# Token sums of batches 1 to 7 as seven block products, with their weights read from DRAM through a ring

## The chip, the cores and the metric

The kernel runs on one core of a Trainium2 chip. The core has a matrix engine (PE; its weight loads are listed apart as PEld), a vector engine (DVE), a scalar engine (ACT), a general engine (POOL, GpSimd), and SP, which here only issues DMAs. Each engine works through its own instructions in order; semaphores make one wait for another. The metric is the time on the device in microseconds (us), the median of several runs.

## The reference

For each of 8 batches of x (3008 tokens, 256 channels, fp32):

```python
# filter
X = np.fft.rfft(x, axis=1)
x = np.fft.irfft(X * (filt_r + 1j * filt_i), n=3008, axis=1)
# mixer
xt = x.transpose(0, 2, 1)
h = np.maximum(xt @ w_tok1, 0.0) @ w_tok2       # 3008 -> 256 -> 3008, over the tokens
u = x + h.transpose(0, 2, 1)
out = u + np.maximum(u @ w_ch1, 0.0) @ w_ch2     # 256 -> 1536 -> 256, over the channels
```

The change concerns `xt @ w_tok1`, the sums over the tokens, for batches 1 to 7.

## The kernel before

**Stages.** The filter is a discrete Fourier transform split into factors (`dft`). It runs for groups of batches, (0), (1, 2), (3, 4), (5, 6), (7); its result goes to DRAM (`g_tmp`) and comes back as six tiles `t4[b, c]` for each batch (`t4_load`), each with 4 of 24 blocks of 128 rows by 256 channels. The blocks are in a space in which one more small transform is still to be done; `w1` holds w_tok1 in that same space, 24 blocks of 128 rows by 256 columns, and stays in SBUF for the whole program.

**The mixer's loop** (`mix`). Its items are (batch, m, jp): m counts 6 groups of up to 512 tokens, jp 6 pairs of blocks of the 1536 hidden channels, so a batch has n = 36 items, 288 in all. An item has three places (0, 1, 2). The up and down products are already made as seven block products each (`up_first`, `up_last`, `down`): sums of the operands on DVE, seven matmuls on PE, sums of the products on ACT and DVE. In place 0 an item issues `up_first` (four matmuls on `ps_pg`, then ACT's copy to `s`), `up_middle` (two adds on DVE), the previous item's `h_sums` (three operations on DVE that write `t`) and the first half of its `down`. In place 1 it issues `up_last` (three matmuls, then DVE's adds into `hh` and ACT's relus), in place 2 the second half of the previous item's `down`, which reads `t`. A finished m adds `finish` to a list of steps (`todo_v`), taken one at a time; the last of these turns the result and stores it with DMAs from POOL (L950).

**The token sums.** At item 32 of a batch (n - 4), place 2, `token_sums(b + 1)` runs 48 matmuls of 128x128 weights by 256 columns into one bank of PSUM (L746), and `token_relu` applies relu on ACT (L754) and has POOL make the five combinations (`combine`) that the second product needs. Their first use is in item 34 (`u_quarter`, L790). Before item 0 of batch 0, `token_sums(0)` does the same for batch 0.

**Around it.** The matmuls of `u_filter` (L768) move 128 columns each. The weights of the second product go to DRAM during batch 0 (`w2_sums` on POOL, one step for each item from item 8) and are loaded for each m again (`w2m_load` on SP, L809). The filter's units for the next group are placed between the mixer's places by a table of due places; their DVE work (L669, L674, L675) and matmuls (L518) lie among the mixer's. They use the two banks `acc` and `b`, as the token sums and the u parts do.

**Order.** The program's order is written out by hand (manual schedule): each engine does its instructions in the order in which they are issued here, and waits come from data and buffers. The pool of the t4 tiles has seven buffers. SP issues most loads, also of the filter's tables and of z.

Of the kernel before, what the change touches and what calls it, by code (L numbers as in the profile page):

```python
# [10 lines left out]
FP32 = mybir.dt.float32  # L11
I64 = mybir.dt.int64
U32 = mybir.dt.uint32
AF = mybir.ActivationFunctionType
ALU = mybir.AluOpType


B = 8
# [5 lines left out]
P = 128  # L24
# [24 lines left out]
W2G = -(-N2 // NG)  # L49
PARTS = (0, 64, 96, 112)  # L50
BY_PE = 6
IN_B = 16
EARLY = 12
GROUPS = ((0,), (1, 2), (3, 4), (5, 6), (7,))
# [71 lines left out]
def kernel(  # L126
# [26 lines left out]
                 for g, bs in enumerate(GROUPS)] for what, shape in (("z", (P, A)), ("g", (K2, KR))))  # L153

    w2_d = nc.dram_tensor("w2_tmp", (MT, P, 7, 256), FP32, kind="Internal").ap()

    def pool(name, bufs, **kw):
        return ctx.enter_context(tc.tile_pool(name=name, bufs=bufs, **kw))
# [38 lines left out]
    filts = [glob.tile([P, 2, KC, D], FP32, name="filt%d" % i) for i in range(FB)]  # L197

    filts_0 = list(filts)
    w1 = glob.tile([P, A, DT], FP32, name="w1")  # L200

    w2 = glob.tile([P, TC, A * P], FP32, name="w2")

# [117 lines left out]

        behind.append(f)

    def w1_load(i):
        st = stage(512)
        rows = moe_w_tok1.rearrange("(n2 n1) t -> n2 n1 t", n1=N1)
        q = nc.sync if i < EARLY else nc.gpsimd
        last = 2 * i + 2 == A
        if last:
            nc.gpsimd.memset(st.bitcast(U32)[HALF:P, 512:1024], 0)  # L330
        for h in range(2):
            n = 1 if last and h else 2
            lo = h * A + 2 * i
            src = rows[:, lo:lo + n, :]
            if h == 0:
                src = bass.AP(tensor=rows.tensor, offset=rows.offset + (A - 1 - lo) * DT,
                              ap=[[N1 * DT, N2], [-DT, n], [1, DT]])
            q.dma_start(st[h * HALF:(h + 1) * HALF, 0:n * DT].rearrange("p (a t) -> p a t", t=DT), src)
        yield

        h = halves(st, 512, spare_pair())
        yield next(h)
        yield next(h)
        on_chip(wai_t, *next(h), 512, [(lambda v: v, w1[:, 2 * i:2 * i + 2, :].rearrange("p a t -> p (a t)"))])

    def w2_load(i):

        t, g = divmod(i, W2G)
        nn = min(NG, N2 - g * NG)
        n = nn * N1  # L350

        st = stage(512)
        nc.gpsimd.dma_start(st[:, 0:n], moe_w_tok2[ts(t, P), ds(g * NG * N1, n)])
        yield
        dst = w2[:, t].rearrange("p (a h n2) -> p h n2 a", h=2, n2=HALF)[:, :, ds(g * NG, nn), :]

        def some(h, first, step, w):
            return (lambda v: bass.AP(tensor=v.tensor, offset=v.offset + first, ap=[v.ap[0], [N1, nn], [step, w]]),
                    dst[:, h, :, 0:w])

        parts = [some(0, A - 1, -1, A), some(1, A, 1, A - 1)]
        if i < BY_PE:
            h = halves(st, n, spare_pair())
            yield next(h)
            yield next(h)
            on_chip(ident, *next(h), n, parts)
        else:
            yield from rounded(st, n, parts, False)

    def combine(w):  # L370
        a11, a12, s4, na22, s3, s2, s1 = (w[:, :, n, :] for n in range(7))
        add = nc.gpsimd.tensor_tensor
        nc.gpsimd.tensor_scalar(out=na22, in0=s1, scalar1=-1.0, scalar2=None, op0=ALU.mult)
        add(out=s1, in0=s3, in1=s1, op=ALU.add)
        add(out=s3, in0=a11, in1=s3, op=ALU.subtract)
        add(out=s2, in0=s1, in1=a11, op=ALU.subtract)
        add(out=s4, in0=a12, in1=s2, op=ALU.subtract)  # L377
# [16 lines left out]
    def wc2_load(i):  # L394
# [11 lines left out]
        while put_off:  # L406
# [4 lines left out]
    LAST = ((wc2_load, 0), (wc1_load, 1), (wc1_load, 4), (wc2_load, 1), (wc1_load, 2), (wc2_load, 2), (wc1_load, 5),  # L411
            (wc2_load, 3), (wc2_load, 4), (wc2_load, 5))

    tiles = ([w1_load(i) for i in range(A // 2)] + [w2_load(i) for i in range(TC * W2G)]
             + [wc1_load(c * (DC // 512), False) for c in range(DH)] + [f(i) for f, i in LAST])
    begin, copy, middle, end = (iter(tiles) for _ in range(4))

# [27 lines left out]
    def copies():  # L445

        while copied[0] < len(tiles) and copied[0] <= ended[0] + 1:
            advance(copy)
            copied[0] += 1
# [292 lines left out]
    def token_sums(b):  # L742
# [4 lines left out]
                                 start=(a == 0 and t == 0), stop=(a == A - 1 and t == TC - 1))  # L747
        return acc

    def token_relu(b, acc):  # L750
        if b:
            h1 = w2[:, 0:1, 7 * 256:].rearrange("p o (s t) -> p o s t", t=P)[:, :, 0:7, :]
            for t, to in enumerate((slice(0, 5, 4), slice(1, 7, 5))):
                nc.scalar.activation(out=h1[:, 0, to, :], in_=acc[:, t].rearrange("p (e i) -> p e i", e=DH), func=AF.Relu)  # L754
            combine(h1)
            return h1[:, 0]
        h1 = h1p.tile([P, TC, D], FP32, tag="h1", name="h1")
        nc.scalar.activation(out=h1, in_=acc, func=AF.Relu)
        return h1
# [86 lines left out]
    def v(out, in0, in1, op=ALU.add):  # L846
        nc.vector.tensor_tensor(out=out, in0=in0, in1=in1, op=op)  # L847
# [127 lines left out]
    def one_step():  # L975
        if todo_v:
            todo_v.pop(0)()

    def mix(next_ready):

        wait = []
        pos, hhs, tts = {}, {}, {}

        def loads(b):
            if b + 1 < B and next_ready(b):
                for c in wait:
                    t4_load(b + 1, c)
                wait.clear()


        own = ({(4, 2): (0, 1)}, {(3, 0): (0,), (4, 0): (1,), (4, 2): (2, 3)})
        new = {(JP - 2, 0): (0, 1), (JP - 1, 0): (2, 3)}

        def u_parts(b, m, jp, place):
            parts = own[b > 0] if m + 1 < MT else new if b + 1 < B else {}
            now = parts.get((jp, place), ())
            b, m = (b, m + 1) if m + 1 < MT else (b + 1, 0)
            for part in now:
                u_part(b, m, part)
            if now and now[-1] == max(p for ps in parts.values() for p in ps):  # L1000
                if m:
                    wait.append(m)
                todo_v.extend(v_steps(b, m))
                if b and (b, m) < (B - 1, MT - 2):
                    w2m_load((m + 2) % MT)

        to_dram = [f for m in range(MT) for f in w2_sums(m)]
        items = [(b, m, jp) for b in range(B) for m in range(MT) for jp in range(JP)]
        n = MT * JP
        for i in range(len(items) + 1):  # L1010
            now, old = i < len(items), i >= 1
            if i and ended[0] < len(tiles):
                convert_middle()
                convert_end(False)
                convert_middle()
            if now:
                b, m, jp = items[i]
                if i % n == 0:
                    wait.append(0)
                w = width(m)  # L1020
                hhs[i] = hp.tile([P, 4, 256], FP32, tag="hh", name="hh")
                g = [bank("pg").rearrange("p (s n) -> p s n", s=2) for _ in range(2)]
                s = up_first(jp, uts[b, m], vts[b, m], w, g)
                up_middle(hhs[i], w, g, s)
            one_step()
            if old:
                bo, mo, jo = items[i - 1]
                tts[i - 1] = tp.tile([P, 4, 256], FP32, tag="t", name="t")
                for f in h_sums(hhs[i - 1], tts[i - 1], width(mo)):
                    f()  # L1030
                down(mo, jo, 0, hhs[i - 1], tts[i - 1], pos.setdefault((bo, mo), []))
            if now:
                u_parts(b, m, jp, 0)
            copies()
            yield b, i % n, 0
            if ended[0] < len(tiles):
                if i == 0:
                    convert_middle()
                convert_end(False)
            if now:  # L1040
                up_last(jp, uts[b, m], vts[b, m], w, g, s, hhs[i])
            one_step()
            if now and i % n == n - 1:
                one_step()
            copies()
            loads(b)
            yield b, i % n, 1
            if old:
                down(mo, jo, 1, hhs.pop(i - 1), tts.pop(i - 1), pos[bo, mo])
                if jo == JP - 1:  # L1050
                    todo_v.extend(finish(bo, mo, uts[bo, mo], pos[bo, mo]))
                    one_step()
                    one_step()
            if now:
                if b + 1 < B and i % n == n - 4:
                    h1s[b + 1] = token_relu(b + 1, token_sums(b + 1))
                u_parts(b, m, jp, 2)
                if jp == JP - 1:
                    while todo_v and m + 1 == MT:
                        one_step()  # L1060
                if i >= 8 and to_dram:
                    to_dram.pop(0)()
                if i in (28, 29):
                    w2m_load(i - 28)
            loads(b)
            yield b, i % n, 2
        while todo_v:
            one_step()
# [125 lines left out]
```

## Time and profile before

| what | value |
|---|---|
| median of three runs (lowest, highest) | 2458.51 us (2456.95, 2459.57) |
| the profiled execution: its time, its span | 2459.61 us, 2457.5 us |
| granted TensorE clock, mean over the span | 0.996 |
| token sums of batches 1 to 7 (L746), first matmul to the next other one, each | 20.7 us |
| DVE's busy share | 75% |
| DMA: moved in all, mean rate | 234.50 MB, 95 GB/s |

The page gives each engine's busy time as a share of the span, the chain of work that ended last, and the costliest groups of instructions with their mean duration and the idle time in front of them. A row of the timeline is: start, length in us, engine, line, operation, what is written and read, shape and count, and in brackets the idle time before it with what ended it. An fp32 matmul stands in the records as two passes, each with a weight load of its own, so the 48 matmuls of a block are 96 records.

### The profile page before, as it was taken

How to read it: one execution, taken by the hardware profiler on the slowest of the kernel's cores; microseconds unless marked ns; L12 is line 12 of the kernel's file. 1: busy time of each engine (PE TensorE's matmuls, PEld its weight loads, DVE VectorE, ACT ScalarE, POOL GpSimd, SP SyncE). 2: the span in 40 equal slices, each digit the busy share in tenths (PEclk: the TensorE clock that was granted, in tenths of full speed). 3: DMA queues.
4: the chain of work that ended last, by engine and by line, in shares of the span. 5: the costliest groups of instructions: out<-in, count | busy, mean ns of one | idle time of the engine just before them, and what ended most of it. 6: DMA issues, size and time to landing. Idle time of an engine off the chain costs nothing.

```text
span 2457.5 us, 33961 instructions
## 1 busy us (share of the span) xinstructions
PE 2413.4 (98%) x11836; PEld 1967.7 (80%) x11836; DVE 1845.0 (75%) x3404; ACT 685.1 (28%) x1348; POOL 601.5 (24%) x1091
## 2 busy tenths in 40 slices
PE   7999999999999999999999999999999999999998
PEld 4767766978788877887888878897888888898887
DVE  7797788587876788578875887857785788757776
ACT  5733222132222222123221222213221222212222
POOL 8483322122112211211211122112212112112121
PEclk8999999999999999999999999999999999999999
DMA  9974434353332232245332322323322121201100
GB/s 217 245 231 130 128 114 137 107 160 107 111 89 59 74 85 57 88 126 159 97 92 57 86 80 73 103 58 116 102 63 73 50 71 47 96 24 30 39 15 20
DMA packets 173842, 234.50 MB, mean 95 GB/s; under 512 B 34013, under 2 KB 123819, under 8 KB 173672
## 3 DMA queue, kind: packets, MB, share of 16 engines
q1 hardware_dynamic: 128856, 174.02, 24.1%
q0 software_dynamic: 33216, 48.32, 7.8%
q10 hardware_dynamic: 11600, 10.00, 1.3%
q8 instruction: 94, 1.54, 0.3%
q14 instruction: 76, 0.62, 0.1%
HBM read 154.99 MB, written 77.22 MB: 94 GB/s over the span
## 4 chain that ended last, share of the span: by engine, by line
PE 88%; DVE 6%; DMA 3%; issue 1%; ACT 1%; POOL 0%; DVEq 0%; ACTq 0%; SPq 0%; POOLq 0%
PE ps_po L903 33%; PE ps_pg L869 18%; PE ps_pg L885 14%; PE ps_b L746 3%; PE ps_acc L746 3%; PE ps_b L518 3%; PE ps_b L790 3%; PE ps_acc L790 2%; PE ps_acc L518 2%; PE ps_b L768 2%; PE ps_acc L768 2%; DVE t L847 1%; DVE hh L847 1%; DVE p L669 1%; DVE u L847 1%
## 5 line engine op out<-in xcount | busy, mean ns | idle before, releaser
L950 POOL DMA_DIRECT2D out_dram<-r x752 | 409.6, 553 | 1646.5 <-ACT hh L890 1433.7
L847 DVE TENSOR_TENSOR hh<-ps_pg,s 128x512 f32<-128x512 f32 (+3 forms) x864 | 482.4, 586 | 384.3 <-ACT s L872 379.8
L890 ACT ACTIVATE hh<-hh 128x512 f32<-128x512 f32 (+1 forms) x576 | 347.8, 621 | 963.1 <-DVE hh L847 956.3
L903 PE MATMUL ps_po<-t,wc 128*128 128x256 f32 (+1 forms) x2304 | 546.5, 380 | 4.6 <-DVE t L847 3.5
L903 PEld LDWEIGHTS ps_po<-t,wc 128*128 128x128 f32 x2304 | 426.5, 190 | 129.8 <-DVE t L847 44.1
L903 PE MATMUL ps_po<-hh,wc 128*128 128x256 f32 (+1 forms) x1728 | 414.0, 375 | 1.4 <-POOL wc L377 0.8
L869 PE MATMUL ps_pg<-v,wc 128*128 128x256 f32 (+1 forms) x1728 | 413.5, 375 | 0.1
L903 PEld LDWEIGHTS ps_po<-hh,wc 128*128 128x128 f32 x1728 | 326.4, 190 | 42.7 <-ACT s L872 3.9
L869 PEld LDWEIGHTS ps_pg<-v,wc 128*128 128x128 f32 x1728 | 326.8, 190 | 40.9 <-DVE v L847 2.9
L885 PE MATMUL ps_pg<-u,wc 128*128 128x256 f32 (+1 forms) x1152 | 295.2, 379 | 0.6 <-DVE hh L847 0.6
L885 PEld LDWEIGHTS ps_pg<-u,wc 128*128 128x128 f32 x1152 | 214.9, 190 | 57.5 <-DVE hh L847 23.7
L847 DVE TENSOR_TENSOR t<-t,hh 128x256 f32<-128x256 f32 (+1 forms) x576 | 245.1, 426 | 19.8
L847 DVE TENSOR_TENSOR s<-ps_pg,hh 128x512 f32<-128x512 f32 (+1 forms) x288 | 196.1, 681 | 31.4 <-DVE hh L847 1.8
L872 ACT COPY s<-ps_pg 128x256 f32<-128x256 f32 (+1 forms) x288 | 106.0, 368 | 330.4 <-PE ps_pg L869 327.6
L847 DVE TENSOR_TENSOR t<-hh 128x512 f32<-128x512 f32 (+1 forms) x288 | 194.9, 677 | 0.6 <-ACT hh L890 0.6
L869 PE MATMUL ps_pg<-u,wc 128*128 128x256 f32 (+1 forms) x576 | 171.7, 380 | 3.4 <-DVE hh L847 3.3
L885 PE MATMUL ps_pg<-v,wc 128*128 128x256 f32 (+1 forms) x576 | 168.8, 375 | 0.0
L869 PEld LDWEIGHTS ps_pg<-u,wc 128*128 128x128 f32 x576 | 106.8, 190 | 35.5 <-DVE hh L847 20.1
L885 PEld LDWEIGHTS ps_pg<-v,wc 128*128 128x128 f32 x576 | 109.2, 190 | 12.6
L847 DVE TENSOR_TENSOR u<-ps_b,u 128x256 f32<-128x256 f32 (+2 forms) x102 | 58.3, 572 | 67.3 <-PE ps_b L790 61.8
L847 DVE TENSOR_TENSOR u<-ps_acc,u 128x512 f32<-128x512 f32 (+2 forms) x108 | 62.4, 577 | 55.8 <-PE ps_acc L790 51.5
L746 PE MATMUL ps_b<-t,w 128*128 128x256 f32 x384 | 85.3, 385 | 1.9 <-DMA t<-g_tmp 1.9
(135 smaller groups left out, 2483.4 us busy)
## 6 DMA issues: line engine op xcount, KB each, us to landing
w<-w_tmp SPq DMA_DIRECT2D x35, 896.0 KB
out_dram<-r POOLq DMA_DIRECT2D x696, 32.0 KB, 2.4
t<-g_tmp SPq DMA_DIRECT2D x42, 512.0 KB
g_tmp<-t SPq DMA_DIRECT2D x96, 192.0 KB
t<-z_tmp SPq DMA_DIRECT2D x180, 96.0 KB
z_tmp<-t SPq DMA_DIRECT2D x60, 256.0 KB
filt<-in_x_dram SPq DMA_DIRECT2D x90, 128.0 KB
wb<-wbi_t SPq DMA_DIRECT2D x64, 128.0 KB
```

What stands on the lines that cost most here:

```text
L518: nc.tensor.matmul(outs(i, j), stat(i, j), mov(i, j), start=True, stop=True)
L669: nc.vector.tensor_tensor(out=prods[c, h], in0=pss[h].unsqueeze(1).to_broadcast([P, 2, nb, D]), in1=filts[c % FB][:, :, 0, :].unsqueeze(2) ...
L746: nc.tensor.matmul(acc[:, t, :], w1[:, a, ts(t, P)], t4[b, a // TC4][:, a % TC4, :], start=(a == 0 and t == 0), stop=(a == A - 1 and t == ...
L768: nc.tensor.matmul(ps[:, ds(q * P, n)], t4[b, c][:, r, ts(dh, P)], wai[:, 0:n], start=(first and q == 0), stop=(not first and q == 3))
L790: nc.tensor.matmul(ps[:, ds(j * hw, hw)], h1[:, n, :], w2m[m % 2][:, at, 0:hw], start=(i < 2 and j == 0), stop=(j == len(todo) - 1))
L847: nc.vector.tensor_tensor(out=out, in0=in0, in1=in1, op=op)
L869: nc.tensor.matmul(ps[:, 0:hw], chan[0][:, jp, n, :], mov, start=True, stop=True)
L872: nc.scalar.copy(out=s[:, 0], in_=g[0][:, 0, 0:hw])
L885: nc.tensor.matmul(ps[:, 0:hw], chan[0][:, jp, n, :], mov, start=True, stop=True)
L890: nc.scalar.activation(out=hs, in_=hs, func=AF.Relu)
L903: nc.tensor.matmul(po[i][:, j, 0:hw], chan[1][:, jp, n, :], mov, start=(jp == 0 and first == 1), stop=(jp == JP - 1 and last == 1))
L950: q.dma_start(bass.AP(tensor=ob.tensor, offset=ob.offset + row * D + g * cw, ap=[[N1 * D, 32], [D if h else -D, n], [1, cw]]), blocks[ts(g ...
```

## The change

For batches 1 to 7 the token sums are formed as 12 steps. A step j takes two blocks of rows of the tokens (2j and 2j + 1), in two halves of channels each, and the two times two 128x128 blocks of `w1` that belong to them, and makes seven products of 128x128 by 128 columns (`token_product`) in place of four of 128x128 by 256, which are eight of 128. Four of the moving operands are sums made on DVE (`t4_sums`, three operations for a step, into a tile with two slots that comes from the pool of the t4 tiles); steps 0 and 1 are issued in place 1 of item 32, step j + 2 right after the matmuls of step j. The products add up over the steps in parts of both banks `acc` and `b`, and at the end ACT copies one part and four DVE operations combine the parts into a tile `c` (from the pool of `r`), before ACT's two relus and POOL's `combine` as before.

The seven weight blocks of a step are in DRAM (`w1_tmp`): from item 8 of batch 0 on, `w1_sums` writes the unchanged blocks out, makes the four combinations in place with 16 operations on POOL, and writes these. They come back through a ring of seven slots in the place that `w1` had (`w1_load`, SP): seven in items 25 to 31, one in place 1 of each, and the last five inside the product, each after the step whose slot it takes. Batch 0 still uses `token_sums`.

```diff
@@ -49,6 +49,8 @@
 W2G = -(-N2 // NG)
 PARTS = (0, 64, 96, 112)
 BY_PE = 6
+AP = A // 2
+W1S = 7
 IN_B = 16
 EARLY = 12
 GROUPS = ((0,), (1, 2), (3, 4), (5, 6), (7,))
@@ -153,6 +155,7 @@
                  for g, bs in enumerate(GROUPS)] for what, shape in (("z", (P, A)), ("g", (K2, KR))))
 
     w2_d = nc.dram_tensor("w2_tmp", (MT, P, 7, 256), FP32, kind="Internal").ap()
+    w1_d = nc.dram_tensor("w1_tmp", (AP, P, 7, P), FP32, kind="Internal").ap()
 
     def pool(name, bufs, **kw):
         return ctx.enter_context(tc.tile_pool(name=name, bufs=bufs, **kw))
@@ -197,7 +200,9 @@
     filts = [glob.tile([P, 2, KC, D], FP32, name="filt%d" % i) for i in range(FB)]
 
     filts_0 = list(filts)
-    w1 = glob.tile([P, A, DT], FP32, name="w1")
+    w1_all = glob.tile([P, W1S * 7 * P], FP32, name="w1")
+    w1 = w1_all[:, 0:A * DT].rearrange("p (a t) -> p a t", t=DT)
+    w1_ring = w1_all.rearrange("p (r s t) -> p r s t", s=7, t=P)
 
     w2 = glob.tile([P, TC, A * P], FP32, name="w2")
 
@@ -321,7 +326,7 @@
 
         behind.append(f)
 
-    def w1_load(i):
+    def w1_tile(i):
         st = stage(512)
         rows = moe_w_tok1.rearrange("(n2 n1) t -> n2 n1 t", n1=N1)
         q = nc.sync if i < EARLY else nc.gpsimd
@@ -411,7 +416,7 @@
     LAST = ((wc2_load, 0), (wc1_load, 1), (wc1_load, 4), (wc2_load, 1), (wc1_load, 2), (wc2_load, 2), (wc1_load, 5),
             (wc2_load, 3), (wc2_load, 4), (wc2_load, 5))
 
-    tiles = ([w1_load(i) for i in range(A // 2)] + [w2_load(i) for i in range(TC * W2G)]
+    tiles = ([w1_tile(i) for i in range(A // 2)] + [w2_load(i) for i in range(TC * W2G)]
              + [wc1_load(c * (DC // 512), False) for c in range(DH)] + [f(i) for f, i in LAST])
     begin, copy, middle, end = (iter(tiles) for _ in range(4))
 
@@ -747,13 +752,71 @@
                                  start=(a == 0 and t == 0), stop=(a == A - 1 and t == TC - 1))
         return acc
 
+    def w1_sums():
+
+        w = w1.rearrange("p (j r) (t n) -> p j r t n", r=2, n=P)
+        to = w1_d.rearrange("j p s n -> p j s n")
+
+        def raw_out():
+            nc.gpsimd.dma_start(to[:, :, 0], w[:, :, 0, 0])
+            nc.gpsimd.dma_start(to[:, :, 1:3], w[:, :, 1])
+
+        def pool(out, in0, in1, op):
+            return lambda: nc.gpsimd.tensor_tensor(out=out, in0=in0, in1=in1, op=op)
+
+        todo = [raw_out]
+        for j in range(0, AP, 3):
+            c11, c21, c12, c22 = (w[:, j:j + 3, r, t] for r in range(2) for t in range(2))
+            todo += [pool(c22, c21, c22, ALU.add), pool(c21, c11, c21, ALU.subtract),
+                     pool(c11, c22, c11, ALU.subtract), pool(c12, c12, c11, ALU.subtract)]
+
+        def sums_out():
+            nc.gpsimd.dma_start(to[:, :, 3:7], w.rearrange("p j r t n -> p j (r t) n"))
+
+        return todo + [sums_out]
+
+    def w1_load(j):
+        nc.sync.dma_start(w1_ring[:, j % W1S], w1_d[j])
+
+    token_ts = {}
+
+    def t4_sums(b, j):
+        if j == 0:
+            token_ts[b] = t4p.tile([P, 2, 4, P], FP32, tag="t4", name="ts")
+        to = token_ts[b][:, j % 2]
+        r = 2 * j % TC4
+        rows = t4[b, 2 * j // TC4][:, r:r + 2].rearrange("p r (e n) -> p (r e) n", e=DH)
+        v(to[:, 0:2], rows[:, 1:4:2], rows[:, 0:2], ALU.subtract)
+        v(to[:, 2], to[:, 1], rows[:, 0])
+        v(to[:, 3], rows[:, 2], to[:, 2], ALU.subtract)
+
+    def token_product(b):
+        one, two = (bank(tag).rearrange("p (s n) -> p s n", n=P) for tag in turn)
+        for j in range(AP):
+            w, t = w1_ring[:, j % W1S], token_ts[b][:, j % 2]
+            r = 2 * j % TC4
+            rows = t4[b, 2 * j // TC4][:, r:r + 2].rearrange("p r (e n) -> p (r e) n", e=DH)
+            todo = ((one, 0, 0, rows[:, 0]), (one, 3, 6, t[:, 0]), (two, 0, 4, t[:, 1]), (one, 2, 3, t[:, 2]),
+                    (two, 1, 2, t[:, 3]), (one, 1, 1, rows[:, 2]), (two, 2, 5, rows[:, 3]))
+            for i, (ps, at, n, mov) in enumerate(todo):
+                nc.tensor.matmul(ps[:, at], w[:, n], mov, start=(j == 0 and i in (0, 2)), stop=(j == AP - 1 and i >= 5))
+            if j + W1S < AP:
+                w1_load(j + W1S)
+            if j + 2 < AP:
+                t4_sums(b, j + 2)
+        c = rp.tile([P, 8, P], FP32, tag="r", name="c")
+        nc.scalar.copy(out=c[:, 0], in_=one[:, 0])
+        v(c[:, 1:3], one[:, 1:3], c[:, 0:1].to_broadcast([P, 2, P]))
+        v(c[:, 3], two[:, 0], c[:, 2])
+        v(c[:, 4:8:3], one[:, 3:4].to_broadcast([P, 2, P]), c[:, 2:4])
+        v(c[:, 5:7], two[:, 1:3], c[:, 3:5])
+        h1 = w2[:, 0:1, 7 * 256:].rearrange("p o (s t) -> p o s t", t=P)[:, :, 0:7, :]
+        for at, to in ((slice(1, 7, 5), slice(0, 5, 4)), (slice(5, 8, 2), slice(1, 7, 5))):
+            nc.scalar.activation(out=h1[:, 0, to, :], in_=c[:, at], func=AF.Relu)
+        combine(h1)
+        return h1[:, 0]
+
     def token_relu(b, acc):
-        if b:
-            h1 = w2[:, 0:1, 7 * 256:].rearrange("p o (s t) -> p o s t", t=P)[:, :, 0:7, :]
-            for t, to in enumerate((slice(0, 5, 4), slice(1, 7, 5))):
-                nc.scalar.activation(out=h1[:, 0, to, :], in_=acc[:, t].rearrange("p (e i) -> p e i", e=DH), func=AF.Relu)
-            combine(h1)
-            return h1[:, 0]
         h1 = h1p.tile([P, TC, D], FP32, tag="h1", name="h1")
         nc.scalar.activation(out=h1, in_=acc, func=AF.Relu)
         return h1
@@ -1005,6 +1068,7 @@
                     w2m_load((m + 2) % MT)
 
         to_dram = [f for m in range(MT) for f in w2_sums(m)]
+        w1_todo = w1_sums()
         items = [(b, m, jp) for b in range(B) for m in range(MT) for jp in range(JP)]
         n = MT * JP
         for i in range(len(items) + 1):
@@ -1042,6 +1106,16 @@
             one_step()
             if now and i % n == n - 1:
                 one_step()
+            if now and i >= 8:
+                for _ in range(2):
+                    if w1_todo:
+                        w1_todo.pop(0)()
+            if now and b + 1 < B:
+                if n - 4 - W1S <= i % n < n - 4:
+                    w1_load(i % n - (n - 4 - W1S))
+                if i % n == n - 4:
+                    for j in range(2):
+                        t4_sums(b + 1, j)
             copies()
             loads(b)
             yield b, i % n, 1
@@ -1053,7 +1127,7 @@
                     one_step()
             if now:
                 if b + 1 < B and i % n == n - 4:
-                    h1s[b + 1] = token_relu(b + 1, token_sums(b + 1))
+                    h1s[b + 1] = token_product(b + 1)
                 u_parts(b, m, jp, 2)
                 if jp == JP - 1:
                     while todo_v and m + 1 == MT:
```

## The prediction

> **What bounds the kernel now.** I read the page's busy line and its chain first, then single rows by form, then the timeline where the change lies.
>
> ```profile
> PE 2413.4 (98%) x11836; PEld 1967.7 (80%) x11836; DVE 1845.0 (75%) x3404; ACT 685.1 (28%) x1348; POOL 601.5 (24%) x1091
> ...
> PE 88%; DVE 6%; DMA 3%; issue 1%; ACT 1%; POOL 0%; DVEq 0%; ACTq 0%; SPq 0%; POOLq 0%
> ```
>
> PE is the bound nearly everywhere, so a microsecond less of matmul is worth a microsecond, and so is every microsecond in which PE newly waits. The sums over the tokens of batches 1 to 7 are seven blocks of 96 records on L746 (two passes per fp32 matmul). The timeline around one of them:
>
> ```profile
> 1020.00 1.15 DVE L847 TENSOR_TENSOR hh<-ps_pg,s 128x448 f32<-128x448 f32 x2
> ...
> 1020.90 20.88 PE L746 MATMUL ps_acc<-t,w 128*128 128x256 f32 x96
> 1021.06 0.70 DVE L935 STREAM_TRANSPOSE r<-u 128x512 f32<-128x512 f32 x1
> ...
> 1041.62 0.54 PE L869 MATMUL ps_pg<-u,wc 128*128 128x224 f32 x2
> ...
> 1041.88 0.66 ACT L754 ACTIVATE w<-ps_acc 128x256 f32<-128x256 f32 x2 [20.12 <-PE ps_acc L746]
> ...
> 1042.63 0.35 ACT L872 COPY s<-ps_pg 128x224 f32<-128x224 f32 x1
> ...
> 1043.01 0.39 DVE L847 TENSOR_TENSOR hh<-ps_pg,s 128x224 f32<-128x224 f32 x1 [21.25 <-ACT s L872]
> ...
> 1043.51 0.62 DVE L847 TENSOR_TENSOR s<-ps_pg,hh 128x448 f32<-128x448 f32 x1
> ...
> 1044.05 0.67 DVE L847 TENSOR_TENSOR t<-hh 128x448 f32<-128x448 f32 x1
> ...
> 1044.27 0.92 PE L885 MATMUL ps_pg<-u,wc 128*128 128x224 f32 x4
> ...
> 1044.75 1.09 DVE L847 TENSOR_TENSOR t<-t,hh 128x224 f32<-128x224 f32 x2
> ...
> 1045.40 1.68 PE L903 MATMUL ps_po<-t,wc 128*128 128x224 f32 x8
> ```
>
> See three things. The block holds PE for 1041.62 - 1020.90 = 20.72 us without a gap, while DVE idles 21 us. DVE is still at work for the item when the block starts (until 1021.76). And what follows has little room: ACT's copy of s, DVE's first add (ends 1043.40) and the next up matmuls (1044.27) stand close behind each other. The other six blocks show the same offsets.
>
> **The matmuls.** 48 matmuls of 256 columns become 12 x 7 = 84 of 128. A pass of 128 columns with new weights each time exists in the kernel, on L768:
>
> ```profile
> 609.04 1.05 PE L768 MATMUL ps_b<-wai,t 128*128 128x128 f32 x8
> ...
> 609.93 1.03 PE L790 MATMUL ps_b<-w 128*128 128x256 f32 x4
> ```
>
> Eight passes take 0.89 us, 111 ns each, against 20.72 / 96 = 216 ns for 256 columns: more than half. So 168 x 0.111 = 18.69 us, a gain of 2.03 us a block (not the eighth, 2.59) and 14.2 us for seven. Bounds: weight loads last 190 ns by their own rows; were they not overlapped, a block took 31.9 us (+11.2). The other end is half of 216, 18.1 us. I take 111, the same form.
>
> **The start of a block.** Each of the 12 steps needs three DVE operations (128x256, 128x128, 128x128), and only one matmul of seven can go before the first. The rows by form:
>
> ```profile
> L847 DVE TENSOR_TENSOR t<-t,hh 128x256 f32<-128x256 f32 x480 | 205.6, 428 | 16.6
> ...
> L847 DVE TENSOR_TENSOR t<-hh 128x512 f32<-128x512 f32 x240 | 165.2, 688 | 0.0
> ```
>
> (688 - 428) / 256 = 1.02 ns an element, so about 298 ns for 128. The sums of steps 0 and 1 are issued on DVE behind the transpose that the timeline shows 0.16 us after the block's start T0, lasting 0.70. They run from T0 + 0.8: first operation done at 1.21, the others at 1.54 and 1.87, step 1 at 2.9. PE does one matmul, waits, loads weights again (0.11) and goes on at 1.37; step 0 ends at 1.37 + 6 x 0.222 = 2.70 in place of 1.55. Cost 1.15 us a block. Bounds: 0 if something I don't see lets DVE come earlier; 1.9 if every one of the three results is waited for.
>
> **Inside a block.** The sums of step j + 2 wait for the matmuls of step j (two slots), start about 0.25 us after their end, need 1.1 us, and first serve 1.55 + 0.22 us after it. That is hidden by step j + 1; without that cover it would be up to 1.35 us on each of ten steps. DVE has nothing else queued: in the old block it idles 21 us. The ring: seven of twelve weight sets (448 KB) are loaded on SP in the seven items before. Five are loaded inside, each when a step ends, each needed six steps (9.3 us) later. In this windows row (columns: stretch, its length, then the engines, clock, DMA share and GB/s) two w loads of 896 KB run alone:
>
> ```profile
> 409.00:413.00 4.00, 4.00 (x22) 3.21 (x21) 0.49 (x2) 1.07 (x3) 0.00 (x0) 1.00 0.99 359
> ```
>
> At 359 GB/s a set takes 1.3 us, less than a step. SP stands behind these waits for some 8 us; what is queued there, the filter's tables and z rows for items 33 on, is two units ahead of use, so I cost it at 0; uncovered it would be the 8 us once a block. The seven earlier loads lengthen SP's queue by 1.3 us per item, within the same lead. The t4 loads lose their spare buffer, since the sums take a seventh one. A load now waits for the u part just issued, but the w load ahead of it on SP waits for that same part: 0.
>
> **The end of a block.** Let T be the start of the matmul after it (1041.62). Before: ACT's two relus from T + 0.26, copy of s at T + 1.01, DVE's add at + 1.39 to + 1.78, up matmuls at + 2.65, t on DVE at + 2.43 to + 3.10, down matmuls at + 3.78. After: ACT copies 128 columns (T + 0.03 to 0.30; the 256-column copies take 372 ns), then four dependent DVE operations of 0.42, 0.29, 0.42, 0.42 (a 256-column add out of PSUM has 421 ns) to T + 1.97, then the relus (starts 0.28 apart), and only then the copy of s, queued behind them on ACT: T + 2.57. DVE's add runs to T + 3.35; the up matmuls go at T + 3.5 (weight load included) and not 2.65, t is done at T + 4.7 and the down matmuls go at 4.8 to 6.35, where they ended at 5.30. Cost 1.05 us. In three of seven blocks the filter's two joins (L674, L675, 0.61 apart) come next on DVE and matmuls (L518) wait for them: 1.35. Bounds: 0.7 (only the first wait counts) and 2.6 (the whole chain). POOL's combine moves from T + 1.0 to T + 2.7, and its result, complete at T + 5.7, is first used after T + 7.9.
>
> A rule against this change: the Trainium skill ("SBUF — State Buffer", section "Who interferes with whom") says that a DVE operation with two SBUF inputs and a GpSimd operation that reads SBUF exclude each other for a whole instruction. The trace shows the combine beside the two t operations, which take 1.09 us in place of 0.82, so 0.14 each and not a whole POOL operation (0.46 to 0.84). By the row the end costs what I wrote; by the rule, with t now under the combine, some 0.5 us more a block, 2465.5 in all.
>
> **Batch 0.** New are 16 POOL operations of 384 columns (some 1.1 us, from 0.73 for 256 on L817), two raw stores and one of sums (5.5 MB) on POOL's queue. POOL waits there for the raw store (15 us, from 256 KB landing in 5.5 us and some overlap); behind it stand the w2 sums and an out store. In the trace POOL idles 28 to 31 us before each such store, so these stay in time. What stays is DVE slowed beside POOL: 1 us, between 0 and 8 (all 17 us of POOL work at the half rate).
>
> **Sum.** -14.2 + 7 x 1.15 + 4 x 1.05 + 3 x 1.35 + 1 = +3.1 us on the profiled execution's 2459.6, which stands 1.1 above the median: about 2462 beside 2458.5.
>
> **The rivals.** (1) Faster: the edges are shorter. For: up matmuls write a half that only ACT reads, so they may not need DVE's add at all. Against: at 429.42 such a matmul starts right as that add ends. The case decides from edges under 1.2 us a block together, where I count 2.3. At 0.4 a block: 2448. (2) The pace of 111 ns does not last: rows show runs of eight only, after slower passes that fill PE's queue; a block has 168. Against: nothing drifts within the eight. At 123 ns a block gains nothing; at 125 the time is 2462 + 16 = 2478. (3) DVE or the ring falls behind inside a block. For: ahead of batch 1's block six t4 loads (3 MB) are issued from 428.2 us, ten before it. Against: the 359 GB/s, by which they are done about when it starts. At 1.3 us a block: 2471. (4) The change lays more on POOL and DMA in batch 0, where DMA is 43 to 50% busy: 8 us, 2469.
>
> **How the numbers follow.** A measurement tells about 0.2%, 4.9 us: 2453.6 to 2463.4. My forecast 0.60, own range 2457 to 2467, of which 0.36 below 2463.4; (1) 0.14; (2) 0.10; (3) 0.08; (4) 0.08, a quarter of it within. So faster 0.14, same 0.38, slower 0.48. The range leaves out the far half of (1) and of (2): 2451 to 2476.
>
> **What would show it.** L746 gives way to 168 records of 128x128 in some 19.9 us from T0 to T; one wait of about 1.1 us on DVE right behind the first matmul; up matmuls at T + 3.5 with a wait on DVE; no wait on DMA inside. Wrong would be: passes over 115 ns, a wait in each step, or an end under 2.8 us.

## The result and the profile after

The changed kernel takes 2472.45 us (median; 2471.36 to 2473.60), the kernel before on the same chip 2458.40 us: a ratio of 1.0058, with a 95% interval of 1.004 to 1.0075. It is slower by 14 us. The prediction said 2462, slower by 3. The direction held; the size didn't: the time lies 5 us above the forecast's own range of 2457 to 2467 (chance 0.60), and only the wide range up to 2476, which has room for half of the second rival, takes it in.

The profiled execution of the changed kernel has a span of 2470.8 us, 13.3 us over that of before. The page's busy line and its chain:

```profile
PE 2409.5 (98%) x12340; PEld 1969.5 (80%) x12340; DVE 1946.4 (79%) x3684; ACT 687.0 (28%) x1355; POOL 622.1 (25%) x1110
...
PE 84%; DVE 9%; DMA 3%; issue 1%; ACT 1%; POOL 0%; SPq 0%; DVEq 0%; ACTq 0%
```

PE's busy time falls by 3.9 us (2413.4 before) while the span grows, so PE waits more; in the chain DVE's share rises from 6 to 9%.

To see where, I took the start of the first up matmul of each of the 288 items in both traces and subtracted. The steps in that difference give the terms:

| term | predicted | profile after against before |
|---|---|---|
| up to item 8 of batch 0, where the preparation of the weights starts | 0 | +2.56 |
| item 8 to item 30 of batch 0 | +1 | +6.86 |
| items 30 to 32 of batch 0 | 0 | -1.44 |
| the seven blocks, item 32 to item 33 | -6.16 | -5.94 |
| the seven ends, item 33 to item 34 | +8.25 | +10.97 |
| all else | 0 | +0.30 |
| sum | +3.1 | +13.31 |

The first row is hardly an effect of the change. All of it stands at item 0 already (+2.83), and the profiles of the other kernels below, whose program is the same up to item 0, stand there between -2.4 and +1.6 us. Nor is the third: the difference falls by 1.1 to 1.45 us there in every kernel profiled, also in those without the new product, so it most likely belongs to the one profile of before.

The timeline around the same block as in the prediction, now L802 (it starts at T0 = 1030.69, the matmul after it at T = 1050.55):

```profile
1030.69 0.39 PE L802 MATMUL ps_b<-t,w 128*128 128x128 f32 x2
1030.85 0.70 DVE L998 STREAM_TRANSPOSE r<-u 128x512 f32<-128x512 f32 x1
1031.48 0.38 DVE L910 TENSOR_TENSOR ts<-t 128x256 f32<-128x256 f32 x1
1031.89 0.29 DVE L910 TENSOR_TENSOR ts<-ts,t 128x128 f32<-128x128 f32 x1
...
1031.91 0.49 PE L802 MATMUL ps_b<-ts,w 128*128 128x128 f32 x2 [0.84 <-DVE ts L910]
...
1050.55 0.54 PE L932 MATMUL ps_pg<-u,wc 128*128 128x224 f32 x2
...
1052.14 0.42 DVE L910 TENSOR_TENSOR c<-ps_acc,c 128x256 f32<-128x256 f32 x1
1052.66 0.72 ACT L815 ACTIVATE w<-c 128x256 f32<-128x256 f32 x2 [1.86 <-DVE c L910]
1053.29 0.33 ACT L935 COPY s<-ps_pg 128x224 f32<-128x224 f32 x1
...
1053.64 0.39 DVE L910 TENSOR_TENSOR hh<-ps_pg,s 128x224 f32<-128x224 f32 x1 [1.08 <-ACT s L935]
...
1054.09 1.02 PE L948 MATMUL ps_pg<-u,wc 128*128 128x224 f32 x4 [0.72 <-DVE hh L910]
...
1054.68 0.88 DVE L910 TENSOR_TENSOR t<-hh 128x448 f32<-128x448 f32 x1
...
1055.04 0.84 POOL L381 TENSOR_TENSOR w<-w 128x128 f32<-128x128 f32 x1
...
1055.61 1.78 PE L966 MATMUL ps_po<-t,wc 128*128 128x224 f32 x8
...
1057.27 0.30 PEld L932 LDWEIGHTS ps_pg<-u,wc 128*128 128x128 f32 x2 [0.23 <-DVE hh L910]
```

One wait of PE stands at the start, on DVE's sums. The block then runs to its end without another: 19.86 us in all. At the end ACT's copy of s comes behind the relus, which come behind DVE's four operations on `c`; up matmuls, down matmuls and the next item follow late.

The largest term is in batch 0. Windows rows there (columns as in the prediction: stretch, length, busy time of PE, PEld, DVE, ACT and POOL, clock, DMA share, GB/s), first before, then after:

```profile
260.00:280.00 20.00, 19.39 (x97) 12.85 (x95) 19.05 (x36) 5.61 (x11) 0.00 (x0) 1.00 0.23 65
280.00:300.00 20.00, 20.00 (x99) 13.85 (x96) 16.83 (x25) 6.58 (x12) 13.17 (x22) 1.00 0.71 198
```

```profile
260.00:280.00 20.00, 18.02 (x79) 11.67 (x79) 19.26 (x29) 4.91 (x10) 13.44 (x15) 1.00 0.38 115
280.00:300.00 20.00, 18.88 (x95) 12.22 (x93) 19.55 (x27) 5.35 (x10) 12.02 (x20) 1.00 0.54 141
```

Before, DVE was already busy for 19 of 20 us between 260 and 280, and POOL idle. After, POOL is busy there for 13 us, DVE finishes 29 instructions in place of 36 in the same busy time, and PE is busy for 1.4 us less. That is the reading which the experiments had to test.

### The profile page after: what moved, and what is told of

Read it like the earlier page. It is cut to its first block, busy times and chain, and to the rows that moved or that the text cites. A ratio compares the mean times of both kernels' runs of the same rounds, so it can differ in the third digit from the quotient of the medians.

```text
span 2470.8 us, 35576 instructions
## 1 busy us (share of the span) xinstructions
PE 2409.5 (98%) x12340; PEld 1969.5 (80%) x12340; DVE 1946.4 (79%) x3684; ACT 687.0 (28%) x1355; POOL 622.1 (25%) x1110
## 4 chain that ended last, share of the span: by engine, by line
PE 84%; DVE 9%; DMA 3%; issue 1%; ACT 1%; POOL 0%; SPq 0%; DVEq 0%; ACTq 0%
PE ps_po L966 31%; PE ps_pg L932 18%; PE ps_pg L948 13%; PE ps_b L523 4%; PE ps_b L802 3%; PE ps_acc L853 3%; PE ps_acc L802 2%; PE ps_b L853 2%; DVE t L910 2%; PE ps_b L831 2%; PE ps_acc L831 2%; DVE hh L910 2%; DMA st<-in_moe_w_tok_dram 1%; PE ps_acc L523 1%; DVE s L910 1%
## 5 line engine op out<-in xcount | busy, mean ns | idle before, releaser
L910 DVE TENSOR_TENSOR u<-ps_acc,u 128x256 f32<-128x256 f32 (+1 forms) x84 | 46.2, 550 | 94.0 <-PE ps_acc L853 86.4
L910 DVE TENSOR_TENSOR u<-ps_b,u 128x512 f32<-128x512 f32 (+2 forms) x126 | 74.5, 591 | 28.8 <-PE ps_b L853 26.7
L853 PE MATMUL ps_acc<-w 128*128 128x256 f32 (+1 forms) x336 | 85.2, 376 | 0.0
```

The lines of the kernel that those rows point to most:

```text
L853: nc.tensor.matmul(ps[:, ds(j * hw, hw)], h1[:, n, :], w2m[m % 2][:, at, 0:hw], start=(i < 2 and j == 0), stop=(j == len(todo) - 1))
```

## The experiments

In what follows, "batch 0" with a number is the step of that difference, against the profile of before, from item 8 to item 30 of batch 0 where nothing else is said. Each profile is one execution. To see how far one can be trusted, the changed kernel was run and profiled again:

> The changed kernel itself, once more, so that the other kernels here stand beside it on the same chip. The stretch before item 0 differed by 1 to 5 us between profiles of kernels that have the same instructions there, so its time should be 2468 to 2474 and its start of item 33 in each batch as in the first profile, to 0.1 us, against item 0 less the loss in batch 0.

It takes 2471.42 us, ratio 1.0052 (1.0035 to 1.0069). Its blocks and ends are the same within 0.01 us, its batch 0 costs 9.8 us in place of 6.9. In this profile the granted clock is 0.50 for two stretches of 3.4 us in batch 0, in the first profile for none (windows rows of `changed_again`; the third figure from the end is the clock):

```profile
217.00:228.80 11.80, 11.55 (x49) 7.93 (x47) 10.02 (x19) 3.41 (x6) 1.16 (x3) 1.00 0.28 78
228.90:232.30 3.40, 3.40 (x9) 2.66 (x9) 2.62 (x4) 0.00 (x0) 3.40 (x7) 0.50 0.54 153
266.50:269.80 3.30, 3.30 (x11) 1.59 (x6) 3.22 (x3) 1.07 (x2) 3.26 (x6) 0.50 0.51 190
```

The items in which they lie, 8 and 12, take 2.4 and 1.4 us longer than in the first profile; 0.9 us of that is made up later. So blocks and ends can be read to a few hundredths of a microsecond, batch 0 to some 3 us, and part of these 3 us is the clock's.

**The preparation alone, and its two halves.** `prep_both` is the kernel before with `w1_sums` added to it; `prep_pool` keeps only the operations on POOL, `prep_dma` only the stores.

```diff
+        w1_todo = w1_sums()
...
+            if now and i >= 8:
+                for _ in range(2):
+                    if w1_todo:
+                        w1_todo.pop(0)()
```

> The kernel before, with the changed kernel's preparation of the weights (the stores and the 16 POOL operations of w1_sums, items 8 to 16 of batch 0) and nothing else of the change; the later batches' token sums then read the combined weights, so they compute something else at the same cost. Theory: of the 14 us that the change costs, what arises in batch 0 comes from this preparation. The profiles of before and after show the start of item 10 at +1.8 us and that of item 25 at +9.4 us. If the preparation does it, item 25 stands about 7 us later than item 10 here too, and the time is 4 to 8 us above before. Rival: the loss in batch 0 comes with the rest (the ring's loads, the lost buffer); then this one is within 2 us of before.

> As prep_both, with the 16 POOL operations alone: no stores of the weights. Theory A (POOL's reads slow DVE's operations with two inputs in SBUF, just where DVE has no slack): most of what prep_both loses, 4 to 6 us. Theory B (the stores' 5.5 MB hold up the filter's loads, so that its work on DVE comes late and in a heap): within 2 us of before.

> As prep_both, with the stores of the weights alone (three DMAs of POOL's queue, 5.5 MB): no POOL operations. Theory A: within 2 us of before. Theory B: most of what prep_both loses, 4 to 6 us.

| kernel | time, us | ratio to before (95%) | batch 0, us |
|---|---|---|---|
| `prep_both` | 2467.20 | 1.0040 (1.0025 to 1.0055) | +9.6 |
| `prep_pool` | 2462.19 | 1.0014 (1.0005 to 1.0024) | +3.6 |
| `prep_dma` | 2459.42 | 1.0002 (0.9993 to 1.0012) | -0.2 |

The preparation accounts for the whole loss in batch 0, by POOL's operations and not by DMA: its stores cost nothing by themselves. But the two halves don't add up to the whole: 3.6 and -0.2 against 9.6. The timeline of `prep_both` shows what the operations do (`w<-w` on L762 are POOL's; the rest is DVE's):

```profile
262.91 0.69 DVE L872 TENSOR_TENSOR s<-ps_pg,hh 128x512 f32<-128x512 f32 x1
262.98 1.96 POOL L762 TENSOR_TENSOR w<-w 128x384 f32<-128x384 f32 x2
263.52 1.98 DVE L872 TENSOR_TENSOR t<-hh 128x512 f32<-128x512 f32 x1
...
265.53 2.90 DVE L872 TENSOR_TENSOR t<-t,hh 128x256 f32<-128x256 f32 x2
...
266.00 2.15 POOL L762 TENSOR_TENSOR w<-w 128x384 f32<-128x384 f32 x2
```

In the profile of before the same two rows last 0.68 and 0.88 us:

```profile
262.54 0.68 DVE L847 TENSOR_TENSOR t<-hh 128x512 f32<-128x512 f32 x1
263.26 0.88 DVE L847 TENSOR_TENSOR t<-t,hh 128x256 f32<-128x256 f32 x2
```

The DVE operation that reads both inputs from SBUF ends only after POOL's pair has ended (263.52 + 1.98 = 265.50, against 264.94), and the next two take 2 us more across the second pair. The one that reads an input from PSUM (`s<-ps_pg,hh`) keeps its 0.69 beside POOL. This agrees with what the Trainium skill ("SBUF — State Buffer", section "Who interferes with whom") says: a DVE operation with two SBUF inputs and a POOL operation that reads SBUF lock each other out for a whole instruction.

Why the stores matter after all is a question of place. In `prep_pool` twelve of the operations lie between 237 and 259 us, the other four between 293 and 300. With the raw store in front, the first of them waits until it is done and starts at 249; eleven then fall between 249 and 268, five between 295 and 304. The profile of before has DVE busy for 11.2 us in 240 to 260, and for 19.05 in 260 to 280 (rows of before, then of `prep_both`):

```profile
240.00:260.00 20.00, 20.00 (x99) 14.43 (x98) 11.23 (x18) 5.45 (x10) 6.80 (x10) 1.00 0.49 154
```

```profile
260.00:280.00 20.00, 16.68 (x72) 10.64 (x72) 19.22 (x28) 4.54 (x9) 9.41 (x12) 1.00 0.33 99
```

The lock acts in the first stretch as well: `t<-hh` takes 1.09 and 1.48 us there in `prep_pool`. But DVE can mostly make up for it there; in the second stretch it can't, and PE waits (busy for 16.7 of 20 us in `prep_both`, 19.4 before). That place decides is so far a reading of these rows; the kernels that move the operations, below, test it.

**The start of the block.** `early_sums` issues the sums of steps 0 and 1 one place earlier.

```diff
                 u_parts(b, m, jp, 0)
+            if now and b + 1 < B and i % n == n - 4:
+                for j in range(2):
+                    t4_sums(b + 1, j)
             copies()
...
-                if i % n == n - 4:
-                    for j in range(2):
-                        t4_sums(b + 1, j)
```

> The changed kernel, with the sums of steps 0 and 1 issued at the end of place 0 of item 32, before DVE's adds of the last up product and the transpose. My step says that a block's start waits about 1.1 us for these sums: the wait behind the first matmul should go, each block with its next matmul is then about 1.0 us shorter (item 32 to 33: 1.9 us less than before in place of 0.86), and the time falls by 7 us against the changed kernel, to about 2465. Rival: DVE is then late with the adds moved behind, and the next item or the last half of the down product waits as long; then the time stays at 2472.

It takes 2463.26 us, ratio 1.0022 (1.0013 to 1.0032). Its timeline around the same block:

```profile
1025.10 0.42 DVE L910 TENSOR_TENSOR ts<-t 128x256 f32<-128x256 f32 x1
...
1026.00 0.38 PE L802 MATMUL ps_b<-t,w 128*128 128x128 f32 x2
...
1026.22 0.39 PE L802 MATMUL ps_b<-ts,w 128*128 128x128 f32 x2
```

The wait is gone: the second matmul follows the first at the pace of the rest. Each block gains 1.89 us on the kernel before in place of 0.85, so the wait had cost 1.04 us a block. The ends don't move (1.42 and 1.91). Seven times 1.04 is 7.3 us; the time fell by 9.2 against the first runs of the changed kernel and by 8.2 against `changed_again`. The rest is within what the other stretches differ by from profile to profile (up to item 8: -1.7 here, +2.6 in the changed kernel's; batch 0: +8.7 here, +6.9 there).

**The end of the block.** `late_relus` issues the two relus and POOL's combine after the next item's copy of s.

```diff
+        def relus():
+            for at, to in ((slice(1, 7, 5), slice(0, 5, 4)), (slice(5, 8, 2), slice(1, 7, 5))):
+                nc.scalar.activation(out=h1[:, 0, to, :], in_=c[:, at], func=AF.Relu)
+            combine(h1)
+
+        late_relus.append(relus)
...
                 s = up_first(jp, uts[b, m], vts[b, m], w, g)
+                while late_relus:
+                    late_relus.pop()()
```

> The changed kernel with the two relus and POOL's combine at a block's end issued after the next item's copy of s, so that on ACT the copy stands in front of them. Theory: the end costs 1.4 to 1.9 us a block because the copy stands behind relus that wait for DVE's chain; then DVE's next add starts at T + 2.0 in place of T + 3.1, the up matmuls at T + 2.65 to 2.75 in place of 3.54, and a block's end costs 0.2 to 0.6: some 8 us less than the changed kernel. Rival: DVE's own chain of four operations and POOL's combine beside the t operations are the cost; then the up matmuls move by less than 0.3 us and the time by less than 3 us.

It takes 2463.29 us, ratio 1.0020 (1.0011 to 1.0030), against 1.0052 (1.0035 to 1.0069) of the changed kernel on the same chip. Its timeline, with T = 1048.37:

```profile
1049.38 0.35 ACT L939 COPY s<-ps_pg 128x224 f32<-128x224 f32 x1 [0.77 <-PE ps_pg L936]
...
1049.95 0.42 DVE L914 TENSOR_TENSOR c<-ps_acc,c 128x256 f32<-128x256 f32 x1
1050.29 0.38 DVE L914 TENSOR_TENSOR hh<-ps_pg,s 128x224 f32<-128x224 f32 x1
1050.47 0.72 ACT L817 ACTIVATE w<-c 128x256 f32<-128x256 f32 x2 [0.74 <-DVE c L914]
...
1051.02 0.92 PE L952 MATMUL ps_pg<-u,wc 128*128 128x224 f32 x4
...
1052.15 1.73 PE L970 MATMUL ps_po<-t,wc 128*128 128x224 f32 x8
```

The copy of s is back at T + 1.01, the up matmuls go at T + 2.65 and the down matmuls at T + 3.78, exactly as in the kernel before. What is left of the loss is 0.10 us in four blocks, 0.66 in one and 1.1 in two; the seven ends cost 3.3 us in place of 11.0. So the queue on ACT was the cause, and not the length of DVE's chain by itself. (The edit moves POOL's combine too, but the up matmuls wait, through DVE's add, for the copy and not for the combine.) What makes the three ends dearer than the others was not tried; the prediction had put the filter's joins there.

**Both edges.** `both_edges` has the two edits together.

> The changed kernel with both: the sums of steps 0 and 1 in place 0 and the relus behind the copy of s. If the edges are separate, the gains add: 7 us and 8 us, so some 15 us below the changed kernel, and below the kernel before by 0 to 3 us in spite of 8 us lost in batch 0. If DVE's lag only moves from one edge to the next, it is not more than 10 us below the changed kernel.

It takes 2457.53 us, ratio 0.9997 (0.9988 to 1.0007): even with the kernel before. Blocks -1.89 and ends +0.10 to +1.11 as in the two single runs, so the gains add. Batch 0 still loses 7.7 us. That is what is left to win.

**The preparation moved.** `prep_moved` is `both_edges` with the raw store in item 1, POOL's operations in item 5 and the store of the sums in item 8. `raw_later` has the raw store in item 4.

```diff
-            if now and i >= 8:
-                for _ in range(2):
-                    if w1_todo:
-                        w1_todo.pop(0)()
+            for f in {1: [raw_out], 5: w1_todo, 8: [sums_out]}.get(i, ()):
+                f()
```

> As both_edges, and the raw store of the weights issued in item 1, the 16 POOL operations together in item 5, the store of the sums in item 8. In the profile before, POOL waits from 193.7 to 210.8 us with nothing to do and DVE is busy 5.6 us in 10 there, against 9.5 in 10 between 260 and 280, where these operations fall in the changed kernel. Theory (POOL's reads cost time only where DVE has no slack): batch 0 loses 0 to 2.5 us in place of 8, and the time is 6 to 8 us below both_edges, 2448 to 2453. Rival (each POOL operation costs its part wherever it lies): within 2 us of both_edges.

> As prep_moved (sums of steps 0 and 1 early, relus late), with the store of the raw weights in item 4, behind the last weight load on POOL's queue, the 16 POOL operations in item 5 and the store of the sums in item 8 as there. Theory: the 5.1 us that PE lost between items 3 and 4 were the weight load that stood behind that store (ACT waited 8.3 us for it); with the store behind the load they go, the POOL operations cost about 1 us as in prep_moved, and the time is 2450 to 2453, some 5 us under prep_moved and 0.2 to 0.35% under the kernel before. Rival: the wait only moves; POOL's operations now wait for the store, slide into items 7 to 9 where DVE has little slack, and cost 4 to 6 us there; the time stays within 2 us of prep_moved, about 2456.

`prep_moved` takes 2456.91 us, ratio 0.9992 (0.9983 to 1.0001). From item 4 to item 30 it loses only 1.1 us, so POOL's operations can be nearly free. But it loses 5.5 us between items 3 and 4, where the others lose nothing. Its waits there (engine and line, what it waited for, us in total, times, longest):

```profile
ACT both L276 <- DMA st<-in_moe_w_ch_dram: 9.6, 2, 8.3
...
PE ps_b L530 <- ACT t L539: 5.1, 1, 5.1
```

The raw store stands on POOL's queue ahead of a load of weights. ACT waits 8.3 us for that load, and PE 5.1 us for what ACT has behind it. The profiled execution is the fastest of the ten, 3.2 us under their median, so the 1.1 us may be somewhat more in the others.

`raw_later` puts the store behind the last such load. The 5 us between items 3 and 4 are gone, and the time is no better: 2456.64 us, ratio 0.9994 (0.9985 to 1.0003). The rival held: the wait moved. POOL now waits for the store and its 16 operations fall together at 205.8 to 223.8 us. Windows rows of `raw_later` (columns as above; the last three figures are the granted clock, the DMA share and GB/s):

```profile
215.00:220.00 5.00, 4.64 (x20) 3.25 (x18) 3.89 (x8) 1.99 (x5) 4.76 (x5) 1.00 0.33 113
220.00:225.00 5.00, 2.83 (x8) 1.77 (x9) 4.93 (x6) 0.32 (x1) 4.76 (x7) 0.83 0.15 50
223.40:226.70 3.30, 3.05 (x8) 2.14 (x7) 2.44 (x4) 1.23 (x2) 1.76 (x4) 0.50 0.11 25
226.80:230.00 3.20, 3.20 (x16) 2.84 (x15) 2.46 (x5) 0.37 (x1) 0.00 (x0) 1.00 0.27 76
230.00:233.50 3.50, 2.29 (x9) 0.76 (x9) 3.04 (x6) 1.23 (x2) 0.32 (x1) 1.00 0.46 127
233.60:236.90 3.30, 3.30 (x9) 2.03 (x7) 2.94 (x4) 0.00 (x0) 3.30 (x7) 0.50 0.52 137
```

DVE is full between 220 and 225 and PE stands for 2.2 us. Items 7 and 8 lose 7.8 us together. The granted clock is 0.50 there in two stretches of 3.4 us; if PE's work takes twice its time in them, up to 3.4 of the 7.8 us are the clock's. That is an estimate from these rows; it leaves 4.4, within the rival's 4 to 6, for the rest.

**Where DVE has room.** `sums_spread` deals the 16 operations out over stretches in which DVE has room. `sums_on_dve` does the same work at the same places on DVE.

```diff
-            for f in {4: [raw_out], 5: w1_todo, 8: [sums_out]}.get(i, ()):
+            for f in {4: [raw_out], 10: w1_todo[:4], 11: w1_todo[4:6], 16: w1_todo[6:10], 17: w1_todo[10:12],
+                      22: w1_todo[12:], 23: [sums_out]}.get(i, ()):
```

> As raw_later (raw store in item 4), but the 16 POOL operations are dealt out over items whose stretch in the profile of both_edges shows DVE with room (4.5 to 7.5 of 10 us busy): four in item 10, two in 11, four in 16, two in 17, four in 22; the store of the sums in item 23. Theory: a POOL operation costs time only where DVE has no room to make up for the operation that it holds off by up to 1 us; so batch 0 loses 1 to 3 us from item 4 to item 31 in place of 8, and the time is 2450 to 2454. Rival: what counts is that four come at once, in any stretch, since PE waits for t at the first held operation: some 2 us for each group of four, 6 to 8 us in all, 2456 to 2458.

> As sums_spread, item for item, but the 16 operations run on DVE (some 0.42 us each, 6.7 us in all, from 1.02 ns an element) and POOL does none of them. If the loss in batch 0 is DVE and POOL keeping each other out, DVE's t operations keep their 0.68 and 0.44 us beside them, and batch 0 loses at most 1 us where sums_spread loses 1 to 3: 2449 to 2453. If it is the load that batch 0 carries (DMA, or any work on a full DVE), putting the work on DVE is no better than sums_spread, or worse by up to the 6.7 us: 2453 to 2458.

`sums_spread` takes 2452.47 us (2449.63 to 2453.09), beside 2459.16 for the kernel before: ratio 0.9974 (0.9964 to 0.9985). In its profile batch 0 loses nothing any more (-0.1 from item 4 to item 30), with the same 16 operations on POOL at the same 1.0 us each. That execution is the fastest of the eight, 2.8 us under their median; by the ratios of `both_edges` and this kernel some 5.7 us of the 7.7 are won. In its timeline the first four operations fall into a time in which DVE waits for ACT anyway:

```profile
246.55 4.22 POOL L765 TENSOR_TENSOR w<-w 128x384 f32<-128x384 f32 x4
...
253.84 0.42 DVE L914 TENSOR_TENSOR hh<-ps_pg,s 128x256 f32<-128x256 f32 x1 [7.41 <-ACT s L939]
```

Eleven of the 16 run while DVE does nothing, and one beside an operation that reads PSUM. The four of item 16 run beside the `t` operations and lengthen them (0.68 and 0.88 us without POOL, in the rows of before above), and that item loses 0.7 us:

```profile
296.18 1.07 DVE L914 TENSOR_TENSOR t<-hh 128x512 f32<-128x512 f32 x1
297.28 2.24 DVE L914 TENSOR_TENSOR t<-t,hh 128x256 f32<-128x256 f32 x2
```

So it is not the amount of POOL's work, nor four operations at once, that costs; what they fall beside does. The run shows this for stretches in which DVE stands still; for stretches in which it is busy in part it has only these four. This version beats both kernels.

`sums_on_dve` takes 2453.41 us, ratio 0.9977 (0.9968 to 0.9985), no better than `sums_spread`; batch 0 loses 2.2 us from item 4 to item 30. My expectation of at most 1 us missed, and the time lies at the lower end of the rival's 2453 to 2458. The operations take 0.56 us (median) and not 0.42, since I took the row for 256 elements and not 384, and up to 1.03 us: POOL still has its operations for the second product, so DVE still runs beside it. The two losses in batch 0 are not to be compared closely, since this profile is at its median and that of `sums_spread` is not. With the work placed well, the choice of engine is worth less than these runs can tell apart.

## Why the prediction was right or wrong

**The matmuls: right.** 168 passes at 111 ns were predicted as 18.69 us. `early_sums`, which has no wait at the start, gains 1.89 us on 20.72, so 18.83 us, 112 ns a pass. Rival 2, that this pace doesn't last, falls.

**The start: right.** 1.15 us were predicted from DVE's queue behind the transpose; 1.04 us is what `early_sums` got back. The first sum started at T0 + 0.79, with 0.8 predicted.

**Inside the block: right.** PE shows no wait on DMA or DVE between 1032 and 1050 us, and the other six blocks last as long to 0.1 us. Rival 3 falls. Its 2471 lies nearest to the measured time, but by another cause.

**The end: right in mechanism, too small.** 1.05 us for four blocks and 1.35 for three were predicted; four cost 1.43, one 1.46 and two 1.90, 2.7 us more in all. The up matmuls came at T + 3.54, with 3.5 predicted. What came later was not followed far enough: the first `t` took 0.88 us beside POOL's combine (0.67 before), the down matmuls went at T + 5.06 and not 4.8, and the weight loads of the next item's up matmuls waited 0.23 us for DVE's hh. The next item starts at T + 6.72, where it started at T + 5.30. Rival 1, shorter edges, falls.

**Batch 0: the step that failed.** "What stays is DVE slowed beside POOL: 1 us, between 0 and 8" was measured at 6.9 and 9.8 us in two profiles of the changed kernel, and at 9.6 in `prep_both`. Two things were wrong in how the value was chosen:

- The cost of one meeting. For the end of a block the prediction weighed a row (the two `t` operations beside the combine, 0.14 us more each) against the rule of the Trainium skill and took the row. For batch 0 it did not work out the 1 us at all: 16 operations at the row's 0.14 would have been 2.2. And the row shows POOL operations of 0.46 to 0.84 us that begin and end around short DVE operations, and is no bound for POOL operations of 1 us that follow each other. There the rule held, with 1.98 us for 0.68 and 2.90 for 0.88. The upper bound of 8 us took DVE at half its rate beside POOL; these rows show about a third, and the bound was passed.
- The place. The prediction costed the raw store's wait by what stands behind it on POOL's queue. What it did was to shift the 16 operations, out of a stretch with DVE busy for 11.2 of 20 us into one with 19.05. The prediction looked at POOL's idle time in this stretch and not at DVE's.

Rival 4 had place and size (8 us); its cause, more load on POOL and DMA, was half right: the stores alone cost nothing, POOL's operations do it through DVE.

With the batch 0 term at its upper bound of 8 and the ends as measured, the prediction's sum would have been 3.1 + 7 + 2.7 = 12.8 us; the medians differ by 14.05. That the time still lies in the wide range is luck: its upper end was made for passes slower than 111 ns, which did not come.

## What to carry to other kernels

Before moving work to an idle POOL, look at DVE's busy time in the stretch where it will run, after all the waits ahead of it on POOL's queue: a POOL operation of 1 us cost next to nothing where DVE stood still, and 0.6 us each (9.6 us for 16 in `prep_both`) where DVE was busy nearly throughout with operations that read SBUF twice. When a result is finished by a longer chain than before, look at what is queued behind its last link on an in-order engine, and issue that first; here moving two relus behind one copy gave back 7.7 us. The seven blocks themselves won 13.2 us (7 x 1.89); a wait of 1.04 us at each start and the ends (11.0 us) took all of it, so the edges of a stage that is made shorter have to be costed as closely as its inside.

## What the runs showed of the hardware that I had not expected

- The lock between DVE and POOL depends on the operands: `s<-ps_pg,hh` kept its 0.69 us while POOL worked, `t<-hh` went from 0.68 to 1.98.
- A load issued on POOL's queue behind a store came late: ACT waited 8.3 us in `prep_moved` for a load of weights behind the raw store. The DMA engines were fully busy then (share 1.03 to 1.04 from 170 to 180 us), so the runs do not separate the order on the queue from the load on the engines.
- The granted clock fell to 0.50 in single stretches of 3.4 us: twice in `raw_later` (rows above), after PE had stood for 2.2 us and for 1.2 us. In `prep_both`, where PE stood for 1.5 of 5 us twice in a row (260 to 270 us), it stayed at 1.00. In `changed_again` it fell at 228.9 us although PE had been busy for 11.55 of the 11.8 us before. So PE's standing still does not tell these cases apart, and what sets it off stays open.
